# Two transformer layers, twice, on one Trainium2 core: another order list, other engine choices, other PSUM banks

## The chip, the core and the metric

The kernel runs on one core of a Trainium2 chip. TensorE (PE; its weight loads are shown apart as PEld), VectorE (DVE), ScalarE (ACT), GpSimd (POOL) and SyncE (SP) each run an instruction stream of their own, and streams meet at semaphores. The metric is the device time of one execution in microseconds, given as the median of several runs. Beside it stands one profiled execution with its own time and trace.

## The reference

An attention layer A and an MLP layer B are applied one after the other, and the pair is applied twice with the same weights (`_A_ref` and `_B_ref` below in short form). The sequence has 2048 tokens of 512 features in bfloat16; there are 32 heads of 16 features, and a query sees the 256 keys up to its own.

```python
def A(x, wqkv, wo):                # H = 32, Dh = 16, W = 256
    q, k, v = heads(x @ wqkv)
    scores = einsum("bhqd,bhkd->bhqk", q, k) * Dh ** -0.5
    scores = where(0 <= q_index - k_index < W, scores, -1e9)
    return merge(softmax(scores) @ v) @ wo

def B(x, w1, b1, w2, b2):          # F = 1792
    return gelu(x @ w1 + b1) @ w2 + b2

for _ in range(2):
    x = x + A(layernorm(x), wqkv, wo)
    x = x + B(layernorm(x), w1, b1, w2, b2)
```

## The kernel before, in words

**Tiling.** The two rounds together are 32 token tiles of 128 tokens (`NT`), taken in 16 attention blocks of two tiles (`NB`) and in MLP jobs of two or four tiles (`JOBS`). The activations X stay in SBUF. There are three kinds of work on PE:

- dense products with 512 or 256 columns: Q, K, V and the output projection (`proj`, `kv`, `outproj`), and the two MLP products W1 and W2 (`mlp`); also a few transposes (`layernorm`). The planner calls them kind "f". A *dense step* below is one node of them: one matmul of 512 columns, two of 256, or two of 512 in the early jobs' W1;
- *visits* (`visit`, names `sa<block>_<number>` and `sb`): the scores of 512 columns for four row groups of heads, as 16 or 24 small matmuls, kind "r". Two exps on ACT read the visit's four PSUM banks and write E;
- *PV pairs* (`pv`, names `od<block>_<half>`): E times V, in two steps of 64 or more small matmuls, kind "c".

Going from one kind to another costs PE a little in itself; the planner counts it as `SWITCH`.

**Other engines.** ACT runs the exps and gelus and must load another table when it goes from one to the other. DVE copies products out of PSUM, computes the layernorm, and shares with GpSimd the multiplication of E by the triangular masks (`mask`, 262 of them), the products TM of the normalisation behind PV, and the small addition of epsilon in the layernorm (L739). Copies of Q, V, the transposed tiles and xv may be done by DVE or ACT.

**Order.** Nothing in the program loops at run time. The functions add some 3233 nodes (`_List.add`), numbered as they are added; each has reads, writes, an engine or two alternatives, and a duration for the planner. Three long lists then fix everything: `ORDER` (L418) is the one order in which nodes go to their engines' streams, so each engine's stream is its part of that list; `TURNS` (L599) picks, for each of the 466 nodes with an alternative, the first (0) or the second (1); `BANKS` (L615) gives the PSUM banks of each allocation in turn. `_List.run` (L231) walks through `ORDER`. `_Sched.op` then works out which semaphores an instruction has to wait for, given what its engine already knows. `spread` (L135) moves a second wait of a PE step to an earlier matmul that has none, where it can; those that find none become a wait instruction of their own. `CODE` (in `_List`) holds the planner's constants for the loading of PE's instruction code, with 2.0090 instructions to a matmul; the diff does not touch it.

A heavy GpSimd instruction is put behind the last DVE instruction marked `lock` that stands ahead of it in the order (`behind`).

**Names used in the prediction.** Each PE node below is one step.

| node | what |
|---|---|
| 40, 47 | transposes of token tiles 0 and 1 for block 0 |
| 52, 61 | parts of the Q and K products of block 0, tile 0 |
| 881, 882 | the PV pair od4_1 |
| 970, 974 | visits sa5_2 and sa5_3 |
| 1019, 1020, 1026, 1027 | W1 product m2_3 and m2_5, two matmuls each |
| 1266, 1267 | the PV pair od6_1 |
| 1209 to 1212, 1337 to 1340 | V products v15 and v16, one matmul of 512 columns each |
| 1331 to 1334 | K product k8_1, two matmuls of 256 columns each |
| 1359, 1365 | visits sa7_2 and sa7_3 |

Matmuls appear in the profile under L32, the helper that issues them (transposes under L36), so they are told apart by their tiles: `ps<-QT,KT` is a visit, `ps<-E,Va` is PV, `ps<-xnTB,W_sb` is W1, `ps<-W_sb,gT` is W2. On the other engines, L949 is the exp, L970 the mask, L1040 the product TM, L723 a copy on ACT.

Of the kernel before, what the change touches and what calls it, by code (L numbers as in the profile page):

```python
# [298 lines left out]
def bass_interleave_layers__sliding_block__dense_activation_gelu__prompt_kernel(  # L299
# [78 lines left out]
    with ExitStack() as kctx:  # L378
        S_ = _Sched(nc, kctx)

        def sb(name, shape, dtype=dt.bfloat16):
# [831 lines left out]
```

## Time and profile before

| | |
|---|---|
| median of 3 runs | 449.11 us (448.99 to 449.49) |
| profiled execution, time | 448.51 us |
| profiled execution, first to last instruction (span) | 446.8 us |
| granted TensorE clock | 0.999 |
| ACT busy | 389.4 us, 87% |
| chain that ended last, by engine | PE 78%, ACT 19%, DVE 1%, issue 1% |

The page gives an execution's busy times and its costliest groups of instructions. A group's row has the line, the engine and the operation, the tiles with output before input, the shapes, the count, then the busy time in us and the mean in ns of one, and then the engine's idle time ahead of these instructions with what ended it. The chain of waits goes back from the last instruction, at each step to what released it. "Issue" stands there for time in which an engine waited for nothing that the profile shows. Matmuls overlap, so the lengths of neighbours in PE's timeline add up to more than the time between their starts.

### The profile page before, as it was taken

How to read it: one execution, taken by the hardware profiler on the slowest of the kernel's cores; microseconds unless marked ns; L12 is line 12 of the kernel's file. 1: busy time of each engine (PE TensorE's matmuls, PEld its weight loads, DVE VectorE, ACT ScalarE, POOL GpSimd, SP SyncE). 2: the span in 40 equal slices, each digit the busy share in tenths (PEclk: the TensorE clock that was granted, in tenths of full speed). 3: DMA queues.
4: the chain of work that ended last, by engine and by line, in shares of the span. 5: the costliest groups of instructions: out<-in, count | busy, mean ns of one | idle time of the engine just before them, and what ended most of it. 6: DMA issues, size and time to landing. Idle time of an engine off the chain costs nothing.

```text
span 446.8 us, 19318 instructions
## 1 busy us (share of the span) xinstructions
PE 433.3 (97%) x8762; PEld 231.8 (52%) x8762; DVE 375.5 (84%) x752; ACT 389.4 (87%) x455; POOL 244.3 (55%) x299
## 2 busy tenths in 40 slices
PE   8999999988989999899999999999999999999997
PEld 5554645645544555454545445545455454445664
DVE  6999999999988898879998999889999877685522
ACT  3999999999989989899998999989987999883442
POOL 5656867876786267454556667665238334324320
PEclk9999999999999999999999999999999999999999
DMA  9920000001210122001220012200301102102002
GB/s 263 370 90 4 3 3 3 4 21 31 62 38 1 39 74 71 17 18 47 71 63 4 25 38 73 63 15 1 87 25 46 54 3 73 38 4 60 26 25 95
DMA packets 39903, 22.88 MB, mean 51 GB/s; under 512 B 24588, under 2 KB 39308, under 8 KB 39820
## 3 DMA queue, kind: packets, MB, share of 16 engines
q1 hardware_dynamic: 39404, 21.24, 16.4%
q8 instruction: 69, 1.13, 1.0%
q10 hardware_dynamic: 416, 0.39, 0.3%
q14 instruction: 14, 0.11, 0.1%
HBM read 13.77 MB, written 7.86 MB: 48 GB/s over the span
## 4 chain that ended last, share of the span: by engine, by line
PE 78%; ACT 19%; DVE 1%; issue 1%
PE ps L32 78%; ACT E L949 15%; ACT gT L1107 2%; ACT gT L1115 1%; ACT L949 1%; PE ps L36 0%; DVE E L970 0%; ACT Va L723 0%; DVE X L791 0%; DVE stat L735 0%; ACT L1115 0%; ACT L1107 0%; ACT xnTA L723 0%; ACT xnTB L723 0%; DVE statmv L737 0%
## 5 line engine op out<-in xcount | busy, mean ns | idle before, releaser
L949 ACT ACTIVATE E<-ps 128x1024 bf16<-128x1024 f32 x304 | 285.9, 1053 | 20.0 <-PE ps L32 19.4
L970 POOL TENSOR_TENSOR E<-E,mask 128x512 bf16<-128x512 bf16 (+1 forms) x135 | 144.1, 1081 | 101.3 <-DVE E L970 45.4
L32 PE MATMUL ps<-W_sb,gT 128*128 128x512 bf16 (+2 forms) x462 | 117.1, 374 | 0.5 <-ACT E L949 0.5
L32 PE MATMUL ps<-xnTB,W_sb 128*128 128x512 bf16 (+1 forms) x560 | 111.8, 337 | 0.1
L32 PE MATMUL ps<-xnTA,Wqkv_sb 128*128 128x256 bf16 (+1 forms) x544 | 76.4, 267 | 1.6 <-ACT xnTA L723 0.7
L32 PEld LDWEIGHTS ps<-xnTB,W_sb 128*128 128x128 bf16 x560 | 51.6, 98 | 41.3 <-ACT E L949 2.9
L32 PE MATMUL ps<-QT,KT 32*64 32x320 bf16 (+4 forms) x2976 | 65.6, 258 | 3.0 <-issue 1.1
L791 DVE TENSOR_TENSOR X<-X,ps 128x512 bf16<-128x512 bf16 x63 | 42.3, 674 | 27.8 <-PE ps L32 27.6
L32 PEld LDWEIGHTS ps<-W_sb,gT 128*128 128x128 bf16 x462 | 41.0, 97 | 43.2 <-issue 5.6
L32 PEld LDWEIGHTS ps<-xnTA,Wqkv_sb 128*128 128x128 bf16 x544 | 46.8, 98 | 25.6 <-issue 3.9
L32 PEld LDWEIGHTS ps<-QT,KT 32*64 32x64 bf16 x2976 | 27.8, 103 | 50.4 <-ACT E L949 33.9
L1115 ACT ACTIVATE gT<-ps,b1T 128x512 bf16<-128x512 f32 (+1 forms) x68 | 36.3, 586 | 18.9 <-PE ps L32 18.8
L1104 DVE TENSOR_SCALAR gT<-ps,b1T 128x512 bf16<-128x512 f32 (+1 forms) x72 | 45.0, 650 | 8.9 <-PE ps L32 8.6
L1035 DVE STREAM_TRANSPOSE TT<-ps 128x1024 f32<-128x1024 f32 x32 | 39.9, 1246 | 12.6 <-PE ps L32 11.1
L32 PE MATMUL ps<-E,Va 64*17 64x128 bf16 (+3 forms) x3872 | 46.1, 229 | 3.4 <-ACT E L949 1.2
L970 DVE TENSOR_TENSOR E<-E,mask 128x512 bf16<-128x512 bf16 (+1 forms) x127 | 46.2, 393 | 1.2 <-ACT E L949 0.7
L32 PEld LDWEIGHTS ps<-E,Va 64*17 64x17 bf16 x3872 | 36.8, 85 | 19.5 <-PE ps L32 7.8
L742 POOL TENSOR_TENSOR statmv<-statmv,mhalf 128x1 f32<-128x1 f32 x64 | 36.1, 569 | 18.9 <-DVE statmv L739 17.3
L735 DVE BATCH_NORM_STATS2 stat<-X 128x6 f32<-128x512 bf16 x64 | 43.4, 681 | 2.5 <-DMA X<-in_A_x_dram 1.9
L1079 POOL TENSOR_TENSOR X<-X,b2b 128x512 bf16<-128x512 bf16 x32 | 36.7, 1154 | 15.5 <-DVE E L970 6.4
L865 DVE TENSOR_TENSOR KT<-ps,parmask 128x1024 bf16<-128x1024 f32 x30 | 36.1, 1204 | 2.2 <-PE ps L32 2.1
L32 PE MATMUL ps<-Wo_sb,OT 128*128 128x512 bf16 x128 | 36.2, 380 | 0.1
(56 smaller groups left out, 345.4 us busy)
## 6 DMA issues: line engine op xcount, KB each, us to landing
scr_x<-xs_ SPq DMA_DIRECT2D x44, 128.0 KB, 1.9
W_sb<-in_B_w_dram SPq DMA_DIRECT2D x2, 1792.0 KB, 15.4
xnTB<-scr_x SPq DMA_DIRECT2D x26, 128.0 KB, 2.5
xnTA<-scr_x SPq DMA_DIRECT2D x18, 128.0 KB, 2.4
out_dram<-X SPq DMA_DIRECT2D x15, 128.0 KB, 1.8
Wqkv_sb<-in_A_wqkv_dram SPq DMA_DIRECT2D x4, 256.0 KB, 5.0
X<-in_A_x_dram SPq DMA_DIRECT2D x1, 1024.0 KB, 9.3
Wqkv_sb<-in_A_wqkv_dram SPq DMA_DIRECT2D x1, 512.0 KB, 6.4
```

What stands on the lines that cost most here:

```text
L32: return self.e.matmul(*a, **k)
L735: add("dve", lambda e, B: e.bn_stats(stat6[:, k6, :], X[:, t, :]), 590, reads=["X%d" % t], writes=["st%d" % k6], prio=prio)
L742: add("pool", lambda e, B: e.tensor_tensor(out=statmv[:, k, 1:2], in0=statmv[:, k, 1:2], in1=mhalf[:], op=ALU.pow), 535, reads=["ve%d" % k ...
L791: add("dve", lambda e, B: e.tensor_tensor(out=X[:, t, :], in0=X[:, t, :], in1=ps[:, B[g][0], :], op=ALU.add), d_psum(512), reads=["X%d" % ...
L865: add("dve", lambda e, B, g=g, i=i: e.tensor_tensor(out=KT[:, kb, :, 2 * i : 2 * i + 2, :].rearrange("p a c q -> p a (c q)"), in0=ps[:, B[ ...
L949: add("act", lambda e, B, g_=g_, gi=gi: e.activation(E[:, 2 * gi : 2 * gi + 2, e0 : e0 + 512], ps[:, B[g_][0] : B[g_][0] + 2, :], AF.Exp, ...
L970: op = lambda e, B, Ew=Ew, Mw=Mw: e.tensor_tensor(out=Ew, in0=Ew, in1=Mw, op=ALU.mult)
L1035: add("dve", lambda e, B: e.transpose(TT[:, s].rearrange("p a c q d -> p a (c q d)"), ps[:, B[g][0] : B[g][0] + 2, :].rearrange("p a n -> ...
L1079: add("pool", lambda e, B: e.tensor_tensor(out=X[:, t, :], in0=X[:, t, :], in1=b2b[:], op=ALU.add), 1110, reads=["X%d" % t, "b2b"], writes ...
L1104: add("dve", lambda e, B, g=g, fc=fc: e.tensor_scalar(out=gT[:, fc, 0:M], in0=ps[:, B[g][0], 0:M], scalar1=b1T[:, fc : fc + 1], scalar2=No ...
L1107: add("act", lambda e, B, fcs=fcs: e.activation(gT[:, fcs[0] : fcs[-1] + 1, 0:M], gT[:, fcs[0] : fcs[-1] + 1, 0:M], AF.Gelu_apprx_tanh, sc ...
L1115: add("act", lambda e, B, g=g, fc=fc: e.activation(gT[:, fc, 0:M], ps[:, B[g][0], 0:M], AF.Gelu_apprx_tanh, bias=b1T[:, fc : fc + 1], scal ...
```

## The change

All of the difference lies in the three lists. `ORDER` holds the same node numbers in another order; 124 of its 3233 places hold the same node as before. `TURNS` differs in 169 of 466 places: 109 masks, 25 epsilon additions, 10 copies of Q, 8 of V, 8 of xv, 8 TM products and one transposed tile go to the other engine. Net, GpSimd has 140 masks in place of 135, 21 TM products in place of 19 and 40 epsilon additions in place of 31; ACT has 13 copies of Q in place of 9, 9 of V in place of 13, and one transposed tile fewer. `BANKS` has 510 new entries. The nodes themselves, the buffers and the planner's constants are the same.

The diff, cut to its first lines and to the places that the prediction speaks of:

```diff
@@ -416,219 +416,219 @@
         psb = ps[:].bitcast(dt.bfloat16)
 
         ORDER = [
-            8, 18, 21, 22, 23, 24, 25, 26, 27, 28, 29, 0, 1, 2, 15, 16, 17, 3, 4, 5, 19, 35, 36, 42, 14, 20, 6, 9,
-            10, 11, 43, 37, 38, 44, 39, 40, 45, 90, 46, 91, 92, 83, 41, 52, 47, 84, 85, 93, 64, 48, 94, 49, 58, 61,
-            86, 7, 59, 65, 87, 50, 95, 88, 51, 96, 89, 53, 66, 60, 78, 62, 97, 54, 98, 99, 100, 79, 80, 81, 101, 82,
...
-            963, 1169, 921, 859, 821, 822, 950, 962, 974, 1020, 880, 1026, 928, 975, 823, 976, 874, 875, 1027, 970,
-            879, 881, 1028, 972, 882, 860, 1021, 1300, 883, 884, 971, 984, 985, 956, 964, 986, 957, 958, 1016, 959,
...
-            1307, 1209, 1330, 1331, 1210, 1211, 1266, 1212, 1213, 1354, 1245, 1359, 1336, 900, 1267, 1314, 1268,
-            1337, 1351, 1360, 1150, 1332, 1338, 1339, 1269, 1361, 1333, 1164, 1340, 1356, 1334, 1335, 1362, 1540,
-            1365, 1402, 1403, 1341, 1388, 1367, 1270, 1376, 1404, 1366, 1358, 1389, 1363, 1390, 1431, 1378, 1377,
...
+            18, 21, 19, 0, 1, 2, 20, 15, 8, 22, 9, 10, 11, 14, 3, 23, 24, 25, 26, 16, 27, 4, 5, 6, 17, 35, 36, 42,
+            43, 44, 37, 38, 39, 40, 45, 41, 90, 46, 47, 91, 92, 83, 61, 84, 85, 52, 58, 93, 64, 94, 48, 7, 65, 86,
+            62, 49, 50, 95, 96, 87, 88, 89, 63, 66, 107, 59, 78, 53, 114, 97, 98, 99, 51, 100, 79, 80, 108, 109, 54,
...
+            963, 822, 962, 974, 874, 859, 950, 875, 879, 559, 975, 928, 860, 880, 823, 573, 855, 769, 866, 870, 976,
+            1026, 1027, 1028, 1019, 921, 784, 970, 1020, 1021, 929, 1300, 881, 882, 971, 984, 972, 883, 986, 956,
...
+            1353, 1354, 1266, 1330, 1209, 1210, 1211, 1212, 1149, 1267, 1355, 1359, 1336, 1337, 1338, 1339, 1540,
+            1213, 1331, 1332, 914, 1333, 1334, 1268, 1360, 1674, 1365, 1340, 1675, 1335, 1341, 1361, 1164, 1367,
...
         TURNS = [
-            1, 1, 0, 1, 0, 1, 0, 1, 0, 1, 0, 0, 1, 1, 1, 0, 1, 0, 1, 0, 0, 0, 0, 0, 0, 1, 0, 1, 1, 1, 0, 1, 0, 1, 1,
...
+            1, 1, 0, 1, 1, 1, 0, 1, 0, 1, 0, 0, 1, 1, 1, 0, 1, 0, 1, 0, 0, 0, 0, 0, 1, 0, 1, 1, 1, 0, 1, 1, 1, 1, 0,
...
         BANKS = (
-            "6 4 0 1 7 6 2 5 3 0 7 6 3412 0 7 1256 0 3 6745 0 1 2367 0 5 0167 4 3 4501 2 7 5634 2 0134 6 4523 7 "
...
+            "2 1 5 0 2 6 7 4 3 1 4 0 4523 7 1 4567 2 3 1267 0 5 3412 0 7 5612 7 4 0123 4 7 5623 4 5601 4 7 0123 "
...
         )
```

399 rows, old and new, of tables (BANKS, ORDER, TURNS) are left out of this document.

## The prediction

> **What bounds the kernel now.** I read the page first, then the busy time by stages, then the chain of waits, and last PE's own timeline where that chain leaves PE.
>
> ```profile
> span 446.8 us, 19318 instructions
> ...
> PE 433.3 (97%) x8762; PEld 231.8 (52%) x8762; DVE 375.5 (84%) x752; ACT 389.4 (87%) x455; POOL 244.3 (55%) x299
> ...
> q8 instruction: 69, 1.13, 1.0%
> ...
> L949 ACT ACTIVATE E<-ps 128x1024 bf16<-128x1024 f32 x304 | 285.9, 1053 | 20.0 <-PE ps L32 19.4
> L970 POOL TENSOR_TENSOR E<-E,mask 128x512 bf16<-128x512 bf16 (+1 forms) x135 | 144.1, 1081 | 101.3 <-DVE E L970 45.4
> ...
> L970 DVE TENSOR_TENSOR E<-E,mask 128x512 bf16<-128x512 bf16 (+1 forms) x127 | 46.2, 393 | 1.2 <-ACT E L949 0.7
> ```
>
> PE has 97% of the span, ACT 87%. Which of the two sets the pace differs by stage, so the busy times are cut where the chain changes hands (columns: stretch, length, then busy time of PE, PEld, DVE, ACT, POOL):
>
> ```profile
> 12.00:127.00 115.00, 108.23 (x2652) 62.53 (x2649) 108.54 (x229) 113.69 (x126) 81.56 (x93) 1.00 0.18 57
> 127.00:184.00 57.00, 55.08 (x1213) 27.90 (x1214) 48.66 (x95) 52.04 (x61) 32.88 (x38) 1.00 0.16 42
> 184.00:312.00 128.00, 127.83 (x2503) 65.11 (x2502) 116.56 (x232) 121.43 (x140) 74.82 (x90) 1.00 0.14 37
> 312.00:425.00 113.00, 112.92 (x2180) 57.67 (x2179) 88.84 (x169) 90.04 (x107) 45.99 (x52) 1.00 0.15 41
> ```
>
> From 12 to 127 us ACT is the bound: 113.69 of 115, so at most 1.31 us can be won there without less ACT work. From 184 to 425 us PE is the bound with 127.83 of 128 and 112.92 of 113: 0.25 us of holes in 241. A reordering cannot win anything there, only lose. The holes that are left are in between, and at the start. The chain names them:
>
> ```profile
> 6.11 0.24 PE ps L36 x4
> ...
> 6.37 0.61 ACT xnTA L723
> ...
> 7.03 0.40 PE ps L32 x4
> 7.42 0.22 PE ps L36 x4
> ...
> 12.59 21.19 ACT E L949 x23
> ...
> 126.23 0.84 PE ps L32 x63
> ...
> 127.12 0.46 PE ps L32 x31
> 127.58 0.69 issue
> 128.27 52.07 PE ps L32 x1130
> 180.34 1.12 issue
> 181.46 71.14 PE ps L32 x1206
> ```
>
> Two entries called "issue", 0.69 and 1.12 us, stand between PE steps: PE waits there for nothing that the profile shows. Over 140 to 425 us the second is all that PE's waits hold:
>
> ```profile
> PE ps L32 <- issue: 1.1, 1, 1.1
> ```
>
> I take both for late instruction code. PE's 8762 matmuls and 8762 weight loads, with 81 separate wait instructions that the program's rules give for this list, are 17,605 instructions; divided by the 69 packets of the instruction queue that is 255 each, so those packets look like PE's code. On average one has to last 446.8/69 = 6.5 us. Before the 1.12 us hole it does not (start, length, what, matmuls):
>
> ```profile
> 176.28 0.74 PE L32 MATMUL ps<-E,Va 64*17 64x64 bf16 x64
> 176.95 0.39 PE L32 MATMUL ps<-Wqkv_sb,xv 128*128 128x512 bf16 x1
> 177.27 0.43 PE L32 MATMUL ps<-QT,KT 32*64 32x128 bf16 x24
> 177.63 0.74 PE L32 MATMUL ps<-E,Va 64*17 64x64 bf16 x64
> 178.30 0.39 PE L32 MATMUL ps<-Wqkv_sb,xv 128*128 128x512 bf16 x1
> ...
> 179.18 0.38 PE L32 MATMUL ps<-xnTA,Wqkv_sb 128*128 128x256 bf16 x2
> 179.40 0.38 PE L32 MATMUL ps<-Wqkv_sb,xv 128*128 128x512 bf16 x1
> 179.61 0.38 PE L32 MATMUL ps<-xnTA,Wqkv_sb 128*128 128x256 bf16 x2
> 179.92 0.42 PE L32 MATMUL ps<-QT,KT 32*64 32x256 bf16 x22
> ```
>
> Many small matmuls in a row use up code fast: 64+1+24+64+10+22 = 185 matmuls, 370 instructions, some 1.45 packets in 4.06 us; then PE stops inside a visit, two matmuls short of its 24.
>
> **The change part by part.** Only the three lists differ, so the work is the same. *Totals.* PE keeps its 1629 steps; changes between its three kinds of step go from 360 to 359; ACT's changes of table stay at 17. Up to the PV step at 126 us the ACT list holds the same number of each kind of instruction (108 exps, 10 gelus, 4 Q, 2 V and so on) in both lists: the ACT-bound stage gets 0 cheaper by count. PE's waits go from 677 to 690, the separate wait instructions from 81 to 82. The added waits I cost at 0: one instruction is 1/255 of a packet, and a wait costs when its event is late, which is priced below as a rival.
>
> *Start.* The list of before has PE do the transpose of token tile 0 (node 40), then a Q product that needs ACT's copy of it (52), then the transpose of tile 1 (47). The list of after has 40, 47, 61, 52. In the chain the copy holds PE from 6.37 to 7.03, and the second transpose is 0.22 us of the chain behind it. Moved into the hole it costs nothing: **-0.22 us**. If its normalised tile comes late, 0.
>
> *The hole at 180 us.* Between the first half of that PV pair (node 1266) and the visit that breaks (1365), before has 8 dense steps; after has 11 (1209 to 1212, 1337 to 1339, 1331 to 1334), with the same small matmuls. A dense step takes 0.22 us (179.18 to 179.40 to 179.61), so the code has 3 x 0.22 = 0.65 us longer to come. Bounds: 0 and 1.12; I take **-0.65 us**.
>
> *The hole at 127 us.*
>
> ```profile
> 124.12 1.47 PE L32 MATMUL ps<-xnTB,W_sb 128*128 128x512 bf16 x6
> ...
> 126.23 1.35 PE L32 MATMUL ps<-E,Va 64*17 64x64 bf16 x95 [0.29 <-ACT E L949]
> 128.27 0.55 PE L32 MATMUL ps<-E,Va 64*17 64x256 bf16 x37 [0.69 <-issue]
> ```
>
> Before the PV pair (881, 882) the six W1 matmuls all stand ahead of the last visit; after puts two of them (node 1020) between the visit and the pair. The pair waits 0.29 us for an exp and then 0.69 for code, 0.98 in all; two such matmuls are 2 x 0.22 = 0.43 us, done inside these waits: **-0.43 us**. The detour adds two changes of kind in place of one, about 0.09 us each (179.61 to 179.92 is 0.31 with one in it); that too lies in the waits. Bounds 0 and 0.98. ACT has 57 - 52.04 = 5 us of slack in the stage behind, so the gain is not at once taken back by it.
>
> *Choices of engine.* 169 of 466 differ. Net, 5 masks, 2 products TM and 9 small epsilon adds go from DVE to GpSimd; 4 Q copies go to ACT and 4 V copies come from it. DVE saves 5 x 0.39 on masks; GpSimd gains 5 x 1.08 = 5.4 us. GpSimd is idle for 128 - 74.82 us in the third stage and DVE for 11, so by busy time both are hidden: 0. The banks (510 entries, all new) show their price only through PE's waits, which are near none after 184 us: 0, and a loss if a bank is freed later.
>
> *Sum.* 0.22 + 0.65 + 0.43 = 1.30 us. The profiled execution took 448.51 us (span 446.8), so 447.2 for such a one; the median of the runs is 449.11, which gives **447.8 us**. The most that the holes allow is 0.22 + 1.12 + 0.98 + 1.31 = 3.63 us: 445.5.
>
> **The rivals.** *Nothing is won (449.1).* A packet comes late wherever small matmuls crowd; 109 of 262 masks and most of the order moved, so the holes may only move: 69 packets had two late ones before, and two of about the old size at new places cost the 1.3 again. For it: dense steps that now stand ahead of one PV pair are missing ahead of another. Against it: only crowded places can break, and 184 to 425 us, with as many visits and PV pairs, had none.
>
> *Slower: masks come late from GpSimd.* A mask that takes 0.39 us on DVE takes 1.08 on GpSimd, and PV must wait for it. One margin of before is already thin:
>
> ```profile
> 77.32 2.26 POOL L970 TENSOR_TENSOR E<-E,mask 128x512 bf16<-128x512 bf16 x2
> ```
> ```profile
> 79.85 1.72 PE L32 MATMUL ps<-E,Va 64*17 64x64 bf16 x128 [0.21 <-ACT E L949]
> ```
>
> The GpSimd mask ends at 79.58, PV starts at 79.85. GpSimd in turn waited 45.4 us for DVE's masks (row above). A mask that misses its place by one GpSimd turn stops PE for about 1.1 us. One is paid by the gain; from the second on the kernel is slower, and three make 447.8 + 3 x 1.13 = **451.2 us** (1.13: half of the 2.26 above). Against it: PE's waits of before name no GpSimd mask at all.
>
> ```profile
> L970 DVE TENSOR_TENSOR E<-E,mask x127: 229/415/779, 23.3 to 406.4; 128x512 bf16<-128x512 bf16 x103, 128x256 bf16<-128x256 bf16 x24
> ```
> ```profile
> L1040 DVE TENSOR_TENSOR TM<-TT,Rc x13: 657/684/1650, 102.3 to 394.0; 128x512 bf16<-128x512 f32 x13
> ```
>
> Least, median and most of DVE's own masks and TM products: a few are stretched, one TM by 0.97 us. The Trainium skill, Perfetto Trace Analysis, Optimizing Scalar/DVE Operations, warns that moving work between these two engines may not help because they share an SBUF port, held for a whole instruction; by that, 5 masks and 2 TM moved could hold DVE off for 7 x 1.1 = 7.7 us, and with none of it hidden the sum would be 455.5 us instead of 447.8. The medians speak against a loss each time, the 1650 ns for one now and then.
>
> *All holes close (445.5).* It needs ACT never idle before 127 us.
>
> **How the numbers follow.** Forecast 447.8 (own range 447.0 to 448.2): 0.42. All holes close: 0.05. Nothing won: 0.22. Late masks: 0.31, though the engine choices look harmless, because after 184 us a reordering has 241 us in which it can only lose. About 0.2%, 0.9 us, is what can be told from no change. Faster: 0.42 + 0.05 = 0.47; same 0.22; slower 0.31. The range goes from the bound 445.5 to the slower rival, 451.2.
>
> **What would show it.** Right: no "issue" of 0.5 us or more in the chain near 127 and 180 us, the second transpose at the start ahead of ACT's first copy's end, PE busy for 127.8 of 128 in the third stage again. Wrong: a new "issue" elsewhere in the chain; PE waiting for POOL E or DVE E after 184 us; or a stage from 12 to 127 us that got longer with ACT below 113.

## The result, and the profile after

The median after is 447.57 us (21 runs, 446.71 to 450.05) against 449.38 us before (21 runs, 447.69 to 452.21): a ratio of 0.9964, 95% interval 0.9949 to 0.9979. A second set of runs (`after_again` below) gave 0.9964 again (0.9942 to 0.9986). The change makes the kernel faster by 1.6 us (0.36% of 449.38; the medians themselves are 1.81 apart).

The profiled execution took 447.93 us, 0.58 us less than that of before, so it shows only a part of that gain. From the page of after:

```profile
span 446.2 us, 19244 instructions
...
PE 421.6 (94%) x8688; PEld 230.9 (52%) x8762; DVE 374.5 (84%) x737; ACT 388.5 (87%) x454; POOL 250.1 (56%) x315
...
q8 instruction: 69, 1.13, 1.1%
...
L970 POOL TENSOR_TENSOR E<-E,mask 128x512 bf16<-128x512 bf16 (+1 forms) x140 | 145.1, 1050 | 89.7 <-ACT E L949 32.3
```

PE's 421.6 us are not less work: only 8688 of its 8762 matmuls have a record, while all 8762 weight loads have one. A missing record looks like an idle gap put down to "issue": 49 of the 50 such entries below average 0.16 us. PE's list of waits has to be read with that in mind:

```profile
PE ps L32 <- issue: 8.5, 50, 0.7
PE ps L32 <- ACT E L949: 4.9, 13, 0.7
...
PE ps L32 <- DMA xnTB<-scr_x: 0.9, 1, 0.9
```

Of the 50 "issue" entries one is a real stop, the longest, 0.7 us. No GpSimd mask (POOL E) is in the list; GpSimd has its five masks more (140) at the old price: the median is 1152 ns in both kernels (the mean, 1050 ns against 1081, mixes two sizes of mask). A wait for the transposed tile xnTB is new. The busy times, by the stages of the prediction:

```profile
12.00:127.00 115.00, 104.15 (x2573) 61.84 (x2588) 109.29 (x227) 112.92 (x125) 81.26 (x100) 1.00 0.18 58
...
184.00:312.00 128.00, 124.62 (x2489) 64.25 (x2514) 116.76 (x226) 120.79 (x139) 75.91 (x92) 1.00 0.14 38
```

ACT is a little less busy up to 127 us (112.92 against 113.69). From 184 to 312 us PE lacks 3.38 us of 128, but with 2489 matmul records to 2514 weight loads up to 25 x 0.16 = 4.0 us of such gaps are only missing records, so nothing was lost there that the trace could show. Where the time went stands in PE's timeline (start, length, what, matmuls; in brackets the idle time before and what ended it):

```profile
123.49 0.43 PE L32 MATMUL ps<-QT,KT 32*64 32x64 bf16 x24 [0.31 <-ACT E L949]
124.83 1.46 PE L32 MATMUL ps<-xnTB,W_sb 128*128 128x512 bf16 x6 [0.91 <-DMA xnTB<-scr_x]
...
127.11 1.34 PE L32 MATMUL ps<-E,Va 64*17 64x64 bf16 x94
129.16 0.56 PE L32 MATMUL ps<-E,Va 64*17 64x256 bf16 x38 [0.71 <-issue]
...
180.11 0.43 PE L32 MATMUL ps<-QT,KT 32*64 32x256 bf16 x24
```

The stop at 180 us is gone: visit sa7_3 runs through its 24 matmuls. The stop inside the PV pair od4_1 is still there, 0.71 us in place of 0.69. The pair starts 0.88 us later than before (127.11 against 126.23): 0.26 of that is the start (first exp at 12.85 in place of 12.59), the rest is the new wait for xnTB less what the pair waited for an exp before. So -1.12 at 180 us and +0.88 ahead of it give 0.24 of the 0.6 us between the two spans; the other 0.36 us are spread over places that I did not follow. The chain of waits of after shows where xnTB is held up:

```profile
117.84 3.97 DMA scr_x<-xs_
...
122.24 2.50 DMA xnTB<-scr_x
```

The store of the normalised tile takes 3.97 us there; the median of its 44 is 1.8 in the page.

### What sets the stops: a count of instructions, and when a packet starts

I laid PE's instructions of both kernels (matmuls, weight loads, separate waits) against the 69 instruction packets. PE's stops at 128 and 180 us in before fall on instructions 5567 and 7871 of its stream. The two are 2304 apart, 9 x 256. The one left in after is at 5570, three off, which my count of separate waits may be. So a packet carries 256 instructions, and these stops fall on every 256th (called an *edge* below). The planner counts them so too: `CODE`, the same in both kernels, starts at 194 and goes by 256, which gives edges at 5570 and 7874. Before's PE passes the edge ahead of the 180 us stop at 176.76 us, and the packet starts at 178.96, 2.20 us later; after's passes it at 176.31 and the packet starts at 177.13, 0.81 later. The DMA view of before, from that edge to 178.90 and then from 178.90 to 180.20 (queue: packets, MB, share of the 16 engines):

```profile
q1 hardware_dynamic: 1296, 0.41, 77.1%
...
q1 hardware_dynamic: 551, 0.14, 47.3%
q8 instruction: 1, 0.02, 4.9%
```

The same view of after, from 176.31 to 177.10 and then to 178.30:

```profile
q1 hardware_dynamic: 118, 0.10, 39.7%
...
q1 hardware_dynamic: 466, 0.12, 43.9%
q8 instruction: 1, 0.02, 5.0%
```

In before 1296 packets of activation transfers go ahead of the code packet, in after 118. The theory to test, called 'late packet': a stop comes when the code packet starts about 2 us or more behind the edge before it, and not where the stretch of small matmuls is long. The rivals: the stretch decides (the prediction's view, three dense steps more; 'length of the stretch'); the gain lies in many places or in the engine choices, and not in the stops ('spread').

### The profile page after: what moved, and what is told of

The parts are those of the page before. It is cut to its first block, busy times and chain, and to the rows that moved or that the text cites. A ratio compares the mean times of both kernels' runs of the same rounds, so it can differ in the third digit from the quotient of the medians.

```text
span 446.2 us, 19244 instructions
## 1 busy us (share of the span) xinstructions
PE 421.6 (94%) x8688; PEld 230.9 (52%) x8762; DVE 374.5 (84%) x737; ACT 388.5 (87%) x454; POOL 250.1 (56%) x315
## 3 DMA queue, kind: packets, MB, share of 16 engines
q8 instruction: 69, 1.13, 1.1%
## 4 chain that ended last, share of the span: by engine, by line
PE 61%; ACT 30%; DVE 5%; issue 2%; DMA 2%; SPq 0%
PE ps L32 60%; ACT E L949 19%; ACT gT L1107 4%; ACT gT L1115 3%; ACT L949 2%; ACT L1115 2%; DMA scr_x<-xs_ 1%; DVE stat L735 1%; DMA X<-in_A_x_dram 1%; DMA xnTB<-scr_x 1%; DVE xs_ L754 1%; DVE X L791 1%; DVE xn L745 1%; PE ps L36 0%; DVE gT L1104 0%
## 5 line engine op out<-in xcount | busy, mean ns | idle before, releaser
L949 ACT ACTIVATE E<-ps 128x1024 bf16<-128x1024 f32 x304 | 286.4, 1052 | 21.0 <-PE ps L32 19.8
L970 POOL TENSOR_TENSOR E<-E,mask 128x512 bf16<-128x512 bf16 (+1 forms) x140 | 145.1, 1050 | 89.7 <-ACT E L949 32.3
L32 PE MATMUL ps<-W_sb,gT 128*128 128x512 bf16 (+2 forms) x421 | 106.1, 373 | 6.0 <-issue 4.8
L32 PE MATMUL ps<-xnTA,Wqkv_sb 128*128 128x256 bf16 (+1 forms) x544 | 69.1, 267 | 1.7 <-ACT E L949 0.9
L32 PEld LDWEIGHTS ps<-W_sb,gT 128*128 128x128 bf16 x462 | 39.6, 98 | 44.8 <-issue 6.9
L32 PEld LDWEIGHTS ps<-xnTA,Wqkv_sb 128*128 128x128 bf16 x544 | 47.8, 98 | 19.6 <-ACT E L949 3.7
L970 DVE TENSOR_TENSOR E<-E,mask 128x512 bf16<-128x512 bf16 (+1 forms) x122 | 48.9, 427 | 4.1 <-ACT E L949 3.9
L1040 POOL TENSOR_TENSOR TM<-TT,Rc 128x512 bf16<-128x512 f32 x21 | 22.2, 1058 | 30.2 <-DVE Rc L1038 20.6
```

The costliest lines, as they stand in the source:

```text
L32: return self.e.matmul(*a, **k)
L949: add("act", lambda e, B, g_=g_, gi=gi: e.activation(E[:, 2 * gi : 2 * gi + 2, e0 : e0 + 512], ps[:, B[g_][0] : B[g_][0] + 2, :], AF.Exp, ...
L970: op = lambda e, B, Ew=Ew, Mw=Mw: e.tensor_tensor(out=Ew, in0=Ew, in1=Mw, op=ALU.mult)
L1040: mul = lambda e, B: e.tensor_tensor(out=TM[:, sm].rearrange("p c q a d -> p a (c q) d"), in0=TT[:, s, :, :, :, 0:Dh].rearrange("p a c q d ...
```

## The experiments

Ratios are against the kernel before, run beside it on the same chip. "Stops inside steps" is the sum of the gaps over 0.2 us between PE's weight loads at the edges, in one profiled execution, where they fall inside a step.

| run | ratio (95% interval), or time of the one execution | stops inside steps, us |
|---|---|---|
| before | | 2.23 |
| `before_again` | 448.29 us | 2.29 |
| `b_start` | 448.15 us | 2.49 |
| `b_stretch` | 1.0000 (0.9984 to 1.0016) | 2.48 |
| `b_dma_later` | 0.9999 (0.9980 to 1.0019) | 3.04 |
| after | 0.9964 (0.9949 to 0.9979) | 0.97 |
| `after_again` | 0.9964 (0.9942 to 0.9986) | 1.06 |
| `a_stretch` | 0.9979 (0.9962 to 0.9996) | 0.60 |
| `a_m2_first` | 0.9998 (0.9976 to 1.0021) | 1.64 |

### Three dense steps moved: into the stretch of before, out of that of after

```diff
 b_stretch (ORDER of before)
-1307, 1209, 1330, 1331, 1210, 1211, 1266, 1212, 1213, ... 1150, 1332, 1338
+1307, 1209, 1330, 1266, 1210, 1211, 1212, 1213, ... 1150, 1331, 1332, 1338
 a_stretch (ORDER of after)
-1336, 1337, 1338, 1339, 1540, 1213, 1331, 1332, 914, 1333, 1334, 1268, 1360, 1674, 1365, 1340
+1336, 1337, 1540, 1213, 1331, 1332, 914, 1333, 1268, 1360, 1674, 1365, 1338, 1339, 1334, 1340
```

> The kernel before, with three dense steps (nodes 1210, 1211 and 1331) moved behind the first half of the PV pair od6_1, so that 11 dense steps stand between node 1266 and the visit sa7_3 as in the kernel after; nothing else differs. Theory 'length of the stretch' (the prediction's): the hole of 1.1 us inside sa7_3 shrinks by 0.65 us to 0.4 to 0.5, whatever the DMA does; time ratio to before about 0.9985. Theory 'late packet' (a code packet that starts about 1 us after PE has passed a code boundary is in time, one that starts 2 us late is not, and transfers of activations are what delays it): the hole follows the start of the packet; if it starts 1.0 us after the boundary there is none, if it starts 2.2 us after it 0.5 to 0.7 us stay. Theory 'spread' (the gain of the change lies in many places or in the engine choices): the hole may shrink, but the ratio stays at 1.000.

> The kernel after, with three dense steps (nodes 1338, 1339 and 1334) moved behind the visit sa7_3, so that 8 dense steps stand between node 1266 and that visit as in the kernel before. Theory 'length of the stretch': a hole of 0.65 us or more opens inside sa7_3, ratio to before about 0.998 in place of 0.9964. Theory 'late packet': with the packet at 0.8 to 1.0 us behind its boundary, as in the kernel after, the hole is at most 0.2 us and the ratio stays near 0.9964; only a packet that comes 2 us late opens it. Theory 'spread': ratio near 0.9964.

b_stretch measured 448.95 us against 448.75, no gain. Its visit sa7_3 is whole, but PE now waits 0.52 us earlier, for the exp that the first PV step needs, and 0.28 us for xnTB behind the visit:

```profile
177.03 0.74 PE L32 MATMUL ps<-E,Va 64*17 64x64 bf16 x64 [0.52 <-ACT E L949]
...
181.33 0.57 PE L32 MATMUL ps<-QT,KT 32*64 32x256 bf16 x24
182.18 1.46 PE L32 MATMUL ps<-xnTB,W_sb 128*128 128x512 bf16 x6 [0.28 <-DMA xnTB<-scr_x]
```

a_stretch has the 8 dense steps of before, and by the prediction's view its stop of 0.65 us or more. It has none, and ran at 447.70 us:

```profile
178.68 0.43 PE L32 MATMUL ps<-QT,KT 32*64 32x256 bf16 x24 [0.22 <-ACT E L949]
```

Its code packet starts 1.03 us behind the edge. So after's list does not need the three dense steps when the packet comes this early, and three dense steps brought forward in before's list only trade one wait for another.

### The loads moved instead: `b_dma_later`

```diff
 ORDER of before, DMA issues 1307, 1314, 1315 put behind visit 1365
+for i in (1307, 1314, 1315):
+    PL.nodes[i]["reads"].append("pv6_1_1")
+    PL.nodes[i]["deps"].add(1267)
```

The three transfers now wait for the PV step 1267; PE's own list is that of before.

> The kernel before, with three transfers of block 9's tiles (nodes 1307, 1314, 1315: two loads of xnTA, one store to scratch), which were issued at 175.1 to 177.9 us, put behind the visit sa7_3 in the order and made to wait for the end of the PV pair od6_1 (node 1267); the two loads of xnTB at 176.2 and 176.7 us stay. PE's order is untouched. Theory 'late packet': with half of the transfers gone from that moment the code packet starts 1.0 to 1.5 us after its boundary in place of 2.2, the hole inside sa7_3 goes from 1.12 to 0.0 to 0.4 us, ratio to before 0.997 to 0.999. Theory 'length of the stretch': PE has the same instructions in the same order, so the hole stays at 1.0 to 1.1 us, ratio 1.000. Theory 'spread': ratio 1.000.

```profile
180.95 0.49 PE L32 MATMUL ps<-QT,KT 32*64 32x256 bf16 x24
```

With before's order on PE and only three transfers started later, the packet comes 0.83 us behind the edge and the visit is whole. But the time is 449.34 us against 449.44, where 'late packet' expected a ratio of 0.997 to 0.999 and both rivals 1.000: this execution has stops elsewhere (1.27 us in od4_1, 0.67 in od12_1, 0.60 in od2_1).

Nor does the whole visit show that the moved transfers did it. `before_again` has no stop in sa7_3 either, with nothing changed: there the packet came 0.95 us behind the edge. Its DMA engines were nearly as busy in the 0.94 us behind that edge (second line, from 177.40 us) as those of before in the same stretch (first line, from 176.76 us):

```profile
q1 hardware_dynamic: 502, 0.22, 83.1%
...
q1 hardware_dynamic: 458, 0.21, 78.5%
```

With about the same transfers in flight one packet started by then and the other 1.25 us later. So the transfers alone do not set the lateness, and one execution of b_dma_later can't be told from the chance that gave before_again an early packet.

### The two W1 products of m2_2 ahead of od4_1: `a_m2_first`

```diff
 ORDER of after
-... 970, 1020, 1021, 929, 1300, 881, 882, 971, ... 985, 1016, 999, 1301, 1000, 1017, 1012, ... 884, 968, 1018, 979
+... 970, 1020, 1021, 929, 1300, 1016, 1017, 1018, 881, 882, 971, ... 985, 999, 1301, 1000, 1012, ... 884, 968, 979
```

> The kernel after, with the W1 product m2_2 (nodes 1016, 1017 and its copy 1018, four matmuls, 0.86 us) moved from behind the visit sa5_5 to ahead of the PV pair od4_1, with bank 5 for it. Theory 'length of the stretch': the hole of 0.71 us inside od4_1 closes, ratio to before 0.994 to 0.995. Theory 'late packet': the hole closes in executions in which the packet is late (2 us or more behind its boundary) and there is none to close in the others, as in the run a_stretch; ratio 0.995 to 0.997. Against both: the visit sa5_5 comes 0.9 us later for ACT when there is no hole, which would give the gain back, ratio 0.9964 or a little more.

```profile
127.42 1.47 PE L32 MATMUL ps<-xnTB,W_sb 128*128 128x512 bf16 x6
128.81 1.68 PE L32 MATMUL ps<-E,Va 64*17 64x64 bf16 x132
...
132.00 0.42 PE L32 MATMUL ps<-QT,KT 32*64 32x256 bf16 x16 [0.18 <-ACT E L949]
132.91 1.04 PE L32 MATMUL ps<-xnTB,W_sb 128*128 128x512 bf16 x4 [0.49 <-ACT E L949]
```

The packet is 2.8 us late here, and yet the PV pair runs through its 132 matmuls: 0.9 us more of dense work ahead of it does cover a late packet. PE then waits 0.18 + 0.49 us for exps, 4 us on, which fits the expectation's last sentence: ACT gets its scores later. At 449.20 us against 449.44 the gain of the change does not show; neither theory's ratio held, and the kernel after itself was not run beside these two.

### The code shifted by 32 instructions, and by 256: `b_shift32`, `a_shift32`, `b_shift256`

```diff
 in clear(n), at the start; 131 in place of 16 and no large ones for b_shift256
+for k in range(16 if n == 3 else 0):
+    r = e.matmul(ps[:, 0, 0:8], gT[:, 0, 0:P], zero[:, 0:8], start=True, stop=True)
```

16 more clearing matmuls of 8 columns are 32 PE instructions with their weight loads; 131 in place of 3 are 256.

> The kernel before with 16 more matmuls of 8 columns in the second clearing step at the start, 32 PE instructions that compute nothing new. Theories on code: the places where PE breaks move by 16 matmuls towards the front, in od4_1 from before the 96th matmul of the pair to before the 80th or so, in sa7_3 from before the 23rd to before the 7th, if the packets are late again. Theory that the holes belong to their instructions (banks, operands): they stay at the 96th and the 23rd. Time about 0.5 us longer for the matmuls themselves.

> The kernel before with the three large matmuls of the second clearing step replaced by 131 of 8 columns: 128 matmuls, 256 PE instructions, more than before, eight times the shift of b_shift32. Theory 'code boundaries, every 256 instructions': the boundaries fall on the same steps of the work as in before, so PE breaks, where it breaks, in the same steps (od4_1 before the 96th matmul of the pair, sa7_3 before the 23rd), the code holes sum to 2 to 3 us, and the time is that of before plus the later start, some 2 to 4 us: 451 to 453. Rival, the extra matmuls at the start do the harm themselves: as bad as b_shift32 or worse, 459 us and more.

> The kernel after with the same 16 extra small matmuls as in b_shift32. Theory 'the order of after is laid out around the code boundaries as that of before is': the boundaries fall on other steps, code holes of 6 us and more in the sum, time 453 us or more. Rival, after has dense steps enough everywhere and so does not depend on where boundaries fall: holes of 1 to 2 us, time 448 us.

b_shift32 (its lines 951 and 972 are L949 and L970 of before):

```profile
131.27 1.16 PE L32 MATMUL ps<-E,Va 64*17 64x64 bf16 x79 [0.44 <-ACT E L951]
133.35 0.71 PE L32 MATMUL ps<-E,Va 64*17 64x128 bf16 x53 [0.92 <-issue]
...
186.39 0.31 PE L32 MATMUL ps<-QT,KT 32*64 32x256 bf16 x7
187.37 0.40 PE L32 MATMUL ps<-QT,KT 32*64 32x256 bf16 x17 [0.66 <-issue]
```

b_shift256:

```profile
129.81 1.35 PE L32 MATMUL ps<-E,Va 64*17 64x64 bf16 x95 [0.44 <-ACT E L951]
131.90 0.55 PE L32 MATMUL ps<-E,Va 64*17 64x256 bf16 x37 [0.74 <-issue]
...
183.37 0.42 PE L32 MATMUL ps<-QT,KT 32*64 32x256 bf16 x22
184.19 0.24 PE L32 MATMUL ps<-QT,KT 32*64 32x128 bf16 x2 [0.41 <-issue]
```

With 32 instructions more the PV pair breaks behind matmul 79 in place of 95, and the visit behind 7 in place of 22: 16 and 15 earlier, as 32 instructions are 16 matmuls. With 256 more both break behind 95 and 22 again. That settles where PE can stop: by the count of its instructions, not by which instruction it is. The price is large, in one execution of each: b_shift32 took 458.91 us, some 9.5 us more than before (its granted clock was 0.992, which may be a part of that), and a_shift32 458.81 at a clock of 1.0, some 11 more than after. PE's waits for "issue" in b_shift32 are

```profile
PE ps L32 <- issue: 8.9, 8, 1.7
```

where before had 1.8 us in 2, and in a_shift32

```profile
PE ps L32 <- issue: 18.9, 58, 2.1
```

where after had 8.5 in 50 (both with 74 records missing). b_shift256, at 451.80 us, has a slower start but not those stops. Both lists are laid out around the edges, the one of after no more robustly than that of before.

The same run corrects the theory. Six stops of b_shift32 are over 1 us by the weight loads (1.06 to 1.81 us), and in five of them the packet starts only 0.98 to 1.07 us behind its edge, so not late. What the shift changed there is which work lies between two edges. Over all the stops inside steps at an edge, of all executions, PE goes on 1.2 to 1.7 us behind the packet's end. So the stretch counts as well as the packet: PE stops where its 256 instructions take less time than the packet's lateness, the packet itself (about 1.0 us) and these 1.2 to 1.7 us together.

### The engine choices swapped: `a_choices_b`, `b_choices_a`

```diff
 a_choices_b: after's ORDER and BANKS
-TURNS of after
+TURNS of before
 b_choices_a: before's ORDER and BANKS
-TURNS of before
+TURNS of after
```

> The kernel after with the engine choices (TURNS) of before; order and banks stay. Theories 'length of the stretch' and 'late packet': most of the gain is in the order, ratio 0.995 to 0.999. Theory 'spread' with the choices as the cause: the gain is gone, ratio 1.000 or more. The order was laid out for its own choices, so some new waits of PE for masks or copies are to be expected under all of them: up to 1 us.

> The kernel before with the engine choices (TURNS) of after; order and banks stay. Theories on the code: the hole near 180 us stays at about 1 us, ratio 0.999 to 1.004. Theory 'spread' with the choices as the cause: ratio 0.996 to 0.998.

They took 470.40 us (ratio 1.0509, 1.0462 to 1.0556) and 481.61 us (1.0741, 1.0711 to 1.0771). PE's waits in b_choices_a:

```profile
PE ps L32 <- POOL E L970: 9.4, 7, 4.0
...
PE ps L32 <- DVE E L970: 4.5, 6, 1.6
```

and in a_choices_b

```profile
PE ps L32 <- POOL E L970: 6.8, 7, 2.1
```

The first lost far more than the 1 us of new waits that its expectation allowed, the second is outside every theory's ratio. Neither choices nor order can be given the gain alone; each list of choices fits its own order. A mask on GpSimd in the wrong place stops PE by up to 4.0 us. The swap also moves some of PE's wait instructions and with them the edges; how much of the 5 and 7% is that was not separated. In b_choices_a the granted clock was 0.982 to 0.989 in every execution, a further part of its 7%.

### The start alone: `b_start`

```diff
 ORDER of before
-... 83, 41, 52, 47, 84, ...
+... 83, 41, 47, 52, 84, ...
```

> The kernel before with the transpose of tile 1 (node 47) ahead of the Q product 52, the change's start alone. The prediction: the time from the start of the first transpose to the start of the first visit, 6.19 us before, becomes 5.97 (0.22 less). Rival: the normalised tile comes too late for PE to use the hole, 6.19 as before. The time of the whole cannot tell 0.2 us in one look; the hole in sa7_3 should be there as in before under every theory.

```profile
5.91 0.63 PE L36 MATMUL ps<-ident,xn 128*128 128x128 bf16 x4
6.85 0.40 PE L36 MATMUL ps<-ident,xn 128*128 128x128 bf16 x4 [0.31 <-DVE xn L745]
...
12.11 0.42 PE L32 MATMUL ps<-QT,KT 32*64 32x256 bf16 x16
```

The second transpose waits for its normalised tile. From the first transpose to the first visit it is 6.20 us, where before has 6.18.

### Both kernels once more: `after_again`, `before_again`

> The kernel after, unchanged, for a second profile and a second ratio. Theory 'late packet' with the gain made of fewer and smaller code holes: their sum inside steps is 0 to 1.7 us, with none in sa7_3, against 2.2 to 3.0 in the kernel before and its variants b_stretch, b_dma_later and b_start; a hole in od4_1 only if that packet starts 2 us late; ratio 0.995 to 0.998. Theory 'spread': code holes as in before, the gain elsewhere.

> The kernel before, unchanged, for a second profile. Theory 'late packet': code holes of 2 to 3 us in the sum, in two or three of the steps sa7_3, od4_1, od12_1 and od2_1, each with a packet that starts 2 us or more behind its boundary at that place or just ahead. Theory 'spread': one hole or none.

The code is unchanged. In after_again PE's longest "issue" is 0.2 us, and the PV pair od4_1 is whole; the wait ahead of it is longer, 1.68 us. The profile names a mask for it, but the second load of xnTB lands at 125.49 us, just ahead of the W1 product that reads it, so it is the wait for xnTB again:

```profile
125.58 1.45 PE L32 MATMUL ps<-xnTB,W_sb 128*128 128x512 bf16 x6 [1.68 <-DVE E L970]
...
127.86 1.68 PE L32 MATMUL ps<-E,Va 64*17 64x64 bf16 x132
```

It took 448.66 us in its profiled execution and before_again 448.29, while the medians beside them are 447.51 and 449.37. A single execution can't rank these two kernels.

The table of stops ranks the two lists. Before's list, in five executions (two of its own, three of variants), has 2.23 to 3.04 us inside steps, 2.5 on average; after's list, in four (two of its own, two of variants), has 0.60 to 1.64, 1.07 on average. The difference, 1.4 us, is near the 1.6 that the median gained. But the times of the same executions are 448.75 and 448.43 us on average, only 0.33 us apart: what the stops cost less does not show as time in them. So that after's list has fewer and smaller stops is shown; that they are where the 1.6 us lie is not, and the rival 'spread' stays open. No version tried beats the kernel after.

## Why the prediction was right, and where its steps were not

The forecast was 447.8 us, the median is 447.57, and "faster" held. That the sum came this close is in good part luck: of its three terms the first brought nothing, the second closed in full though it did not need the steps that it counted, and the third was not seen.

*What bounds the kernel: right as far as is shown.* PE's stops were the holes that before's profile had. (That there are none behind 184 us holds for the profiled before, but not always: b_start, b_stretch and b_dma_later have one of 0.40 to 0.67 us between 334 and 337 us.) Taking "issue" for late instruction code was right: the shift experiments move the stops by as many instructions as were added, within one matmul. What the prediction lacked is that the place is fixed by a count (every 256 instructions, as in the planner's `CODE`) and that the packet's lateness changes from one execution to the next; it took only the length of the work into account, which is one half of the condition.

*The start, -0.22: wrong.* Its own "if its normalised tile comes late, 0" is what happens (b_start 6.20 against 6.18 us). In after the whole stretch is 6.44 us, with a further 0.43 us wait for ACT's copy of a later tile, and 6.13 in after_again: about 0, or a loss of 0.26.

*The hole at 180 us, -0.65: right in sign, mis-sized, and its reason was not the deciding one.* It closed wholly, 1.12 us. The three dense steps do lengthen PE's work between the two edges, from 3.41 us in b_dma_later, which has before's order on PE and no stop, to 3.99 in after; that is near the 0.65 of the step. But they were not needed: with 8 steps there is no stop either where the packet comes 0.8 to 1.0 us behind the edge (a_stretch, b_dma_later and the unchanged before_again). What differs between the two profiled executions is the packet, 2.20 us against 0.81. In all four executions of after's list it comes 0.8 to 1.05 us behind this edge; in those of before's list with the transfers in place it comes at 0.95, 1.76, 2.20 and 2.28. So after's order seems to bring it earlier; by what means is not shown.

*The hole at 127 us, -0.43: not shown.* The step put two W1 matmuls into waits of 0.29 and 0.69 us. Their work is there: between the two edges PE takes 3.99 us without its waits, 3.48 before. In the profiled after the second is 0.71, and a new wait of 0.9 us for xnTB stands ahead of it, which no step of the prediction priced. In after_again and a_stretch the pair is whole, with packets 1.62 and 1.17 us behind the edge. In all four executions of after's list and its variants PE waits 0.7 to 1.7 us ahead of m2_5, and such a wait, too, gives a late packet time. Dense work can cover a late packet (a_m2_first), but that took 0.9 us of it, not 0.43.

*Added waits and engine choices at 0: right for this change, and for a thinner reason than given.* No POOL mask stops PE in after. Idle time on GpSimd was named as the cover, but the swaps suggest that the margin at each place is what counts. The Trainium skill, Perfetto Trace Analysis, Optimizing Scalar/DVE Operations, cautions that offloading between DVE and GpSimd may not help because of their shared port. Here DVE's masks take 417 ns at the median in place of 415, but those of 512 columns 443 ns on average in place of 417, 2.8 us over the 108 of them, and the longest 995 ns in place of 779; its longest TM product takes 693 ns in place of 1650. PE waits 0.2 us for DVE's masks in both kernels, so the price of 7.7 us that the prediction worked out from this rule did not reach PE. That the banks are "all new" is not exact, 46 of the 510 are as before; nothing rests on it.

*The rivals.* "The holes only move" was nearer the truth than its chance: they do come and go from one execution to the next, at places fixed by the count, and after's list has fewer of them. "Late masks" did not occur in after, but its mechanism is real at a larger price than 1.13 us each: 9.4 us for 7 in b_choices_a.

*What would show it.* No "issue" of 0.5 us or more near 180 us held, near 127 us it failed. The second transpose does stand ahead of the end of ACT's first copy, but brought no gain. ACT came to 112.92, just under the 113 named as a sign of trouble, in a stage that got longer by the wait of 0.9 us ahead of 124.83. PE's busy time in the third stage can't be compared, as records are missing. The median gained more than the places named in the prediction give in this one execution; where the rest is stays open.

## What to carry to other kernels

Where a stop of an engine has no releaser in the trace, count that engine's instructions between two such stops. Here they were a multiple of 256 apart, which pointed to code loading; then the place of every instruction behind an edit moves too, and 32 added instructions cost far more than their own time. Before adding work to cover such a stop, look at when its code packet started, and in more than one execution. And where the stops vary by more than the change is worth from one execution to the next, rank kernels by medians of many runs and use the trace only to find mechanisms.

## What the runs showed of the hardware that was not expected

- *256 instructions to a packet, and a price for lateness.* A packet of 16 KB (69 of them, 1.13 MB) comes about 1.0 us behind the edge as a rule, takes about 1.0 us, and where PE stopped it went on 1.2 to 1.7 us behind the packet's end. From these figures I estimate that 256 instructions of less than some 3.2 us make PE stop even when the packet is not late. 32 instructions more at the start cost 9.5 to 11 us of 449, in one execution of each kernel.
- *What makes a packet late is open: other transfers alone do not.* The Trainium skill, DMA: Bandwidth & Descriptors, Queues, rings and completion order, says that an engine takes its queues in turn, one packet each. By that a waiting code packet would be served soon; at 178.96 us in before it started behind 1296 packets of the other queue, 81 for each of the 16 engines. Either the order differs, or the profile's packets are smaller than those that the Trainium skill means, or the request itself came late. Two observations speak for the request. In before_again the packet of the same edge came at 0.95 us under nearly the same traffic. And before's packet at 78.17 us started 2.73 us behind its edge (75.44) with no transfer at all between, as the stretches of before show (the last two columns, the DMA engines' share and GB/s, are 0):

```profile
75.40:78.10 2.70, 2.70 (x65) 1.77 (x57) 2.44 (x6) 2.70 (x4) 2.07 (x3) 1.00 0.00 0
```

What delays a packet there stays open, as does whether after's stop in od4_1 could be closed by moving its transfers, which was not tried.
